# A gated long-convolution block and its feed-forward on one core: the filter's first transform turned round, its transposes moved to VectorE, and the front in a new order

## The chip, the cores and the metric

The kernel runs on one core of a Trainium2 chip. It has five engines with queues of their own: TensorE (PE in the profile; its weight loads are PEld), VectorE (DVE), ScalarE (ACT), GpSimd (POOL) and SyncE (SP), which here only issues transfers. Each works through its instructions in the order of the program and waits on semaphores where it needs another's result. The metric is the device time of one execution in microseconds (us), lower is better.

## What is computed

```python
x = A_q                                                   # 1 x 2048 x 512, float32
sa, ca, ga, sb, cb, gb = (silu(c) @ w_mod) in six rows of 512
h  = layernorm(x) * (1 + ca) + sa
ks = causal 4-tap convolution of A_k with A_shift_k, per channel
kv = ks * A_v
y  = irfft(rfft(kv, 4096) * rfft(A_ssm_k, 4096))[:2048] + kv * A_ssm_D
x  = x + ga * (h * y)
h  = layernorm(x) * (1 + cb) + sb
out = x + gb * ((silu(h @ w_gate) * (h @ w_up)) @ w_down) # 512 -> 1792 -> 512
```

There are 2048 tokens and 512 channels. The long convolution runs over tokens, for every channel, with a filter as long as the sequence; it is what the front of the kernel spends most of its time on.

## The kernel before, in words

**Two parts.** The *front* does the modulation rows, the short and the long convolution, the gate and the second normalization, and the first gate and up products; its order is written out by hand as one list of calls, from `load_k0(0)` to `next_psum()`. The *loop* is the feed-forward over 14 blocks of 128 hidden channels and two halves of the tokens, in float32 products split into three passes. The loop begins with the tile called `a`. The helper class `InOrder` keeps every engine's instructions in the order of the list, so the place of a call in the list is its place in the queue of each engine that it uses. All instructions are recorded at one line (L40), and are told apart by their tiles.

**Names.** `c_` or the first number is one of four channel blocks of 128 channels. The long convolution is a product of transforms, done in two steps of a DFT as small matrix products, for the signal X and for the filter K.

- *Short convolution:* `tap0`, `tap`, `tms`, `tma` build `u` from the four taps on ScalarE, VectorE and GpSimd; `times_v` multiplies by v. Channel block 0 arrives in another layout and has its own calls: `x0_taps`, `x0_mul`, `p_tap`, `p_mul`, `p_turn`.
- *First step for X:* `x_turn` turns 8 pieces by TensorE into the tile `kvt`, which ScalarE copies out as `x`. `x_first` multiplies by the constant DFT matrix (`raw`, tile `er`) into PSUM tile `s`, and a copy of 1024 columns stores it into X in fours, interleaved. `swap_x(n)` then turns piece n % 4 of X(n // 4) in place, 32 x 32 blocks, with VectorE's transpose.
- *First step for K:* `skip` adds the direct term D to the filter's first element (tile `ss`), so the term y += kv * D comes out of the same product. `k_first` multiplies the filter by the DFT matrix, here with the filter as the stationary operand (`s<-er,ss`). Two copies of 512 columns per call store it in KT (tile `kt`). `k_turn` then has TensorE transpose eight 128 x 128 pieces against the identity into PSUM tile `kt`, and copies them into K.
- *Second step, product and way back:* `x3` (tile `px`, two parts copied to `xs`), `x_sum` (the third part), `product3(n, m)` (TensorE makes K's second step in tile `pk`, VectorE multiplies `xs` by it), `inv3` or `inv3s` (tile `iv`, back into X; in `inv3s` VectorE's transpose does it). n runs over 8 half blocks, m over 3 parts. X(0) to X(2) are turned by a round trip to DRAM: `put` (away<-X) and `get` (X<-away).
- *Modulation:* `mod_load` brings two rows' weights (`wm`), `mod_mul` scales them by silu(c) on ScalarE, `mod_part` adds them up on GpSimd, `mod_bc` spreads the sums to all partitions by TensorE, `mod_mix` mixes them. The third pair of rows goes by `mod_row`, `mod_out` and `mod_T`.
- *Gate and second normalization:* tokens are in four quarters t. `do_stats`, `gate_n` and `gate_p` (two 512-wide instructions per token row of a partition) make the first h; `y_pe` makes the convolution's output in PSUM; `y_into` or `y_gate` and `add_y` multiply and add it to x, with the statistics of the second normalization. `rs1`, `rs2`, `rs3` finish these (VectorE, GpSimd, GpSimd), `norm1` applies them on ScalarE, `norm_t` transposes (tile `nt`), `norm_s` scales, `hi1` and `lo1` split the result in a high and a low part (tile `op`) for the products `gu_pe` (tile `g`), `gu_act` and `gu_end`.

**Room.** PSUM is handed out in four tiles of two banks (`banks`). The list `SLOTS` says which buffer each allocation takes. KT and the third weights of the modulation take turns in one buffer (`f16`, one tag with one buffer), so KT of the next channel block can be written once the last one has been read. `warm(n)` issues n products of the identity that nobody reads.

Of the kernel before, what the change touches and what calls it, by code (L numbers as in the profile page):

```python
# [43 lines left out]
def adaln_h3_swiglu(ctx, tc, q, k0, v0, kT, vT, ssm, dskip, wgu, wdn, wmod, e_fwd, e_inv, w_c, out):  # L44
# [1186 lines left out]
    room()
    tap(1, 1)
    tap(1, 2)
    skip(0, e=dve)
# [3 lines left out]
    load_v(2)
    swap_x(2)
    swap_x(3)  # L1240
    k_first(0, 2, e=act)
    k_first(0, 1, e=act)
# [1 line left out]
    k_first(0, 3, e=act)
    times_v(1, 1, e=pool)
    k_first(0, 0, e=act)
    tap0(2, e=act)
    warm(5)
    k_turn(0, 0, e=act)
    k_turn(0, 1, e=dve)  # L1250
    tap(2, 1)
    times_v(1, 0, e=pool)
    k_turn(0, 2, e=act)
    x_turn(1, 1, e=act)
    k_turn(0, 3, e=act)
    tap(2, 2)
    load_ssm(1)
# [42 lines left out]
    mod_load(0)  # L1300
    tma(3, 2, 0, e=pool)
    tma(3, 3, 0, e=pool)
    product3(0, 0)
    load_ssm(3)
    mod_mul(0, 0, e=act)
    load_ssm(2)
    product3(1, 2)
    product3(0, 1)
# [494 lines left out]
```

## Time and profile before

| What | us |
|---|---|
| three runs | 573.32, 573.87, 575.27; median 573.87 |
| the profiled execution | 574.47, span 572.7 |
| TensorE busy | 567.3 |
| VectorE busy | 436.9 |
| GpSimd busy | 330.9 |
| ScalarE busy | 301.0 |
| the front, to the loop's first product | 181.4 |

A row of groups reads: line, engine, operation, tile written <- tiles read, partitions x elements, count | busy us, mean ns of one | idle time of the engine before them and what ended it. A float32 product is recorded as two matmul passes, a transpose as one. The ends of matmuls are modelled, and the duration of one (275 ns) overlaps the next; their pace is seen in the starts and in the chain of waits. A row of a timeline reads: start, duration, engine, operation, tiles, count, and in brackets the idle time before it. The chain of waits is followed back from the last instruction, so its rows are the start and the length of each piece of work on it.

### The profile page before, as it was taken

The numbers are of one execution on the slowest core, as the hardware profiler recorded it, in microseconds if no ns is written. First come the engines' busy times: TensorE is split into PE (matmuls) and PEld (weight loads), VectorE is DVE, ScalarE is ACT, GpSimd is POOL, SyncE is SP. The second block draws the span as 40 slices with busy tenths as digits, with TensorE's granted clock in tenths as the row PEclk, the third lists the DMA queues.
The fourth block names the chain that finished last, engine by engine and source line by source line (L and its number), as shares of the span: only waits on it lengthen the run. The fifth ranks groups of instructions, "written<-read, shape, count | busy, mean of one in ns | idle before, by whom it ended". The sixth has DMA issues, their size and how long they took to land.

```text
span 572.7 us, 10192 instructions
## 1 busy us (share of the span) xinstructions
PE 567.3 (99%) x4010; PEld 450.5 (79%) x4010; DVE 436.9 (76%) x625; ACT 301.0 (53%) x459; POOL 330.9 (58%) x303
## 2 busy tenths in 40 slices
PE   9999999999999999999999999999999999999997
PEld 9985476546888888888888888887888888888886
DVE  4897896989998866676576569857686868686766
...
GB/s 318 401 289 228 383 264 240 208 255 208 76 38 201 121 247 168 228 260 62 248 285 380 170 167 0 116 198 166 129 166 129 166 128 166 129 166 129 166 0 147
DMA packets 52545, 108.00 MB, mean 189 GB/s; under 512 B 19345, under 2 KB 34065, under 8 KB 46482
## 3 DMA queue, kind: packets, MB, share of 16 engines
...
## 4 chain that ended last, share of the span: by engine, by line
PE 90%; DMA 3%; ACT 2%; DVE 2%; SPq 1%; issue 0%; POOL 0%; ACTq 0%; POOLq 0%
PE a L40 23%; PE dn L40 15%; PE c L40 12%; PE b L40 6%; PE da L40 6%; PE s L40 4%; PE g L40 4%; PE iv L40 3%; PE pk L40 3%; PE dc L40 3%; PE kvt L40 2%; DMA wm<-in_wmod 2%; PE kt L40 2%; PE px L40 2%; PE warm L40 1%; PE y L40 1%
## 5 line engine op out<-in xcount | busy, mean ns | idle before, releaser
L40 PE MATMUL a<-op,wsum 128*128 128x512 f32 x432 | 109.8, 390 | 0.0
L40 PEld LDWEIGHTS a<-op,wsum 128*128 128x128 f32 x432 | 81.0, 188 | 17.4 <-ACT p L40 0.4
L40 PE MATMUL dn<-wd,acts 128*128 128x512 f32 x336 | 84.8, 389 | 0.0
L40 PEld LDWEIGHTS dn<-wd,acts 128*128 128x128 f32 x336 | 63.1, 188 | 13.1
L40 ACT COPY p<-a 128x512 f32<-128x512 f32 x50 | 29.4, 587 | 57.7 <-PE a L40 57.7
L40 DVE TENSOR_TENSOR x<-x,dn 128x512 f32<-128x512 f32 (+1 forms) x65 | 43.2, 670 | 13.2 <-PE dn L40 12.9
L40 POOL TENSOR_TENSOR wa<-ws,wa 128x512 fp32r<-128x512 f32 (+1 forms) x28 | 32.0, 1165 | 26.2 <-ACT wa L40 26.2
L40 POOL TENSOR_TENSOR tb<-wds 128x256 f32<-128x256 f32 x12 | 8.9, 741 | 62.7 <-DVE wds L40 62.7
L40 ACT COPY r<-a 128x512 f32<-128x512 f32 x24 | 14.1, 587 | 53.8 <-PE a L40 53.8
L40 DVE TENSOR_TENSOR b<-r,c 128x512 f32<-128x512 f32 x24 | 16.7, 696 | 32.2 <-ACT sg L40 32.2
L40 POOL TENSOR_TENSOR wsum<-sr,wsum 128x512 fp32r<-128x512 f32 x28 | 40.1, 1456 | 0.0
L40 PE MATMUL c<-op,wsum 128*128 128x512 f32 x156 | 39.6, 389 | 0.0
L40 PE MATMUL c<-op,wa 128*128 128x512 f32 x156 | 39.6, 389 | 0.0
L40 PE MATMUL b<-op,wa 128*128 128x512 f32 x144 | 36.5, 389 | 0.0
L40 POOL TENSOR_TENSOR wd<-wds,wd 128x512 fp32r<-128x512 f32 x14 | 18.3, 1327 | 30.4 <-ACT wd L40 30.4
L40 PEld LDWEIGHTS c<-op,wa 128*128 128x128 f32 x156 | 29.3, 188 | 6.1
L40 PEld LDWEIGHTS c<-op,wsum 128*128 128x128 f32 x156 | 29.3, 188 | 6.1
L40 DVE TENSOR_TENSOR x<-x,da 128x512 f32<-128x512 f32 x48 | 32.7, 681 | 0.9 <-PE da L40 0.9
L40 DVE TENSOR_TENSOR xs<-pk,xs 128x1024 f32<-128x1024 f32 x24 | 27.6, 1213 | 7.3 <-PE pk L40 7.3
L40 PEld LDWEIGHTS b<-op,wa 128*128 128x128 f32 x144 | 27.0, 188 | 5.6
L40 POOL TENSOR_TENSOR s<-s,bcs 128x512 f32<-128x512 f32 x22 | 28.3, 1299 | 0.9
L40 ACT ACTIVATE sg<-a 128x512 f32<-128x512 f32 x26 | 15.5, 598 | 22.6 <-PE a L40 22.6
...
## 6 DMA issues: line engine op xcount, KB each, us to landing
...
```

Source lines behind the costliest of these rows:

```text
L40: return lambda *a, **k: self.tc.keep_in_program_order(f(*a, **k))
```

## The change

`k_first` exchanges its operands: the DFT matrix is stationary and the filter moves, as in `x_first`. What lies along the partitions of the result changes with it, and it is stored by one interleaved copy of 1024 columns. `k_turn`, with its transposes on TensorE and its copies, is gone; `k_swap(c_, i)` has VectorE transpose 32 x 32 blocks from KT to K instead, four calls of 1024 columns to a channel block. `x_first` is split in four calls of a quarter each; the work in them is the same. The long list of calls has a new order, with some calls on other engines. Calls of `mod_mul` stand on ScalarE in both.

```diff
@@ -51,11 +51,11 @@
     dp = ctx.enter_context(tc.tile_pool(name="dp", bufs=1, space=bass.MemoryType.DRAM))
 
     SLOTS = {
-        "e8": "...",
-        "b16": "...",
+        "e8": "...",
+        "b16": "...",
...
-        "ps": "...",
-        "r4": "...",
+        "ps": "...",
+        "r4": "...",
...
     }
     pps = [
@@ -281,50 +281,41 @@
         x = XT[c_, half] = r4([P, 8, P], F32, f"x{c_}{half}")
         copy(e, x, pt)
 
-    def x_first(c_, half, e=act):
-
-
-        if half == 0:
+    def x_first(c_, jq, e=act):
+
+        if c_ not in X:
             X[c_] = b16(f"X{c_}")
-        x = XT.pop((c_, half))
-        for o in range(0, 8, 4):
-            ps = banks("s1")
-            j0 = 8 * half + o
-            for jj in range(4):
-                for a in range(2):
-                    pe.matmul(
-                        ps[:, a, jj * P : (jj + 1) * P], raw[rows(a), j0 + jj], x[rows(a), o + jj], start=True, stop=True
-                    )
-            copy(e, fours(X[c_])[:, j0 // 4 :: 4], ps.rearrange("p a (f d) -> p a d f", f=4))
-
-
-    def k_first(c_, jq, e=act):
-
-        if c_ not in KT:
-            KT[c_] = f16(f"kt{c_}", (P, 4, 32, 32))
+        x = XT[c_, jq // 2]
         ps = banks("s1")
         for jj in range(4):
             for a in range(2):
                 pe.matmul(
-                    ps[:, a, jj * P : (jj + 1) * P], SS[c_][rows(a), 4 * jq + jj], raw[rows(a), 4 * jq + jj],
+                    ps[:, a, jj * P : (jj + 1) * P], raw[rows(a), 4 * jq + jj], x[rows(a), (4 * jq + jj) % 8],
                     start=True, stop=True,
                 )
-        for a in range(2):
-            j = J * a + 4 * jq
-            copy(
-                e, KT[c_][:, :, j : j + 4, :].rearrange("p g j k -> p j g k"),
-                ps[:, a].rearrange("p (j g k) -> p j g k", j=4, g=4),
-            )
-
-    def k_turn(c_, m, e=act):
-
-        if m == 0:
+        copy(e, fours(X[c_])[:, jq::4], ps.rearrange("p a (f d) -> p a d f", f=4))
+
+    def k_first(c_, jq, e=act):
+
+        if c_ not in KT:
+            KT[c_] = f16(f"kt{c_}", (P, 32, P))
+        ps = banks("s1")
+        for jj in range(4):
+            for a in range(2):
+                pe.matmul(
+                    ps[:, a, jj * P : (jj + 1) * P], raw[rows(a), 4 * jq + jj], SS[c_][rows(a), 4 * jq + jj],
+                    start=True, stop=True,
+                )
+        copy(e, fours(KT[c_])[:, jq::4], ps.rearrange("p a (f d) -> p a d f", f=4))
+
+    def k_swap(c_, i):
+
+        if c_ not in K:
             K[c_] = b16(f"K{c_}")
-        ps = banks("kt").rearrange("p a (k d) -> p (a k) d", k=4)
-        src = KT[c_].rearrange("p g j k -> p (g j) k")
-        for k in range(8):
-            pe.transpose(ps[:, k], src[:, :, 8 * m + k], ident)
-        copy(e, fours(K[c_])[:, 2 * m : 2 * m + 2], ps.rearrange("p (g f) d -> p g d f", f=4))
+        r = slice(32 * i, 32 * i + 32)
+        dve.transpose(
+            fours(K[c_])[:, :, r].rearrange("p g d f -> p d g f"), fours(KT[c_])[:, :, r].rearrange("p g d f -> p d g f")
+        )
 
     def fours(t):
 
```

The new list, in order, from the start to where the loop's buffers are set up. A call without a name behind it runs on its only engine or on ScalarE; the calls behind it (`wd_lo` to `next_psum`) are those of before.

```
load_k0(0); diag(0); warm(5); diag(1); diag(2) DVE; load_dskip(); warm(16); diag(3); load_k0(1); p_tap0() DVE; p_tap(1,1) DVE; p_tap(1,0)
DVE; p_tap(2,0) DVE; load_k(1); p_tap(2,1) DVE; x0_taps(0); p_tap(3,1) DVE; load_v0(0); load_v0(1); x0_mul(0); load_e(0); load_ssm(0,0);
small_in(); silu_c(); tap0(1); load_e(2); load_ssm(0,2); load_e(1); p_tap(3,0) DVE; p_mul(0) DVE; p_mul(1) POOL; x0_taps(1); x_first(0,0);
load_e(3); load_ssm(0,1); p_turn(); skip(0) POOL; tap(1,1); k_first(0,2); x0_mul(1); tap(1,2); tap(1,3); x_first(0,1); x_first(0,3);
x_first(0,2); swap_x(1); load_ssm(0,3); k_first(0,3); load_v(1); times_v(1,0) POOL; k_first(0,0); k_first(0,1); times_v(1,1) POOL;
load_k(2); tap0(2); swap_x(0); load_wc(); swap_x(2); times_v(1,3) POOL; load_ssm(1); times_v(1,2) POOL; k_swap(0,0); k_swap(0,1);
x_turn(1,0); x3(0,2); x3(0,1); x_turn(1,1); x_sum(0) POOL; k_swap(0,3); k_swap(0,2); k_first(1,3); x_first(1,0); x_first(1,1); skip(1) POOL;
swap_x(3); x3(1,1); x3(1,2); tap(2,1); tap(2,2); tap(2,3); load_ssm(3); k_first(1,1); load_k(3); skip(3) POOL; k_first(1,2); x_sum(1) POOL;
load_v(2); x_first(1,2); x_first(1,3); times_v(2,0) POOL; tms(3,2); mod_rep() DVE; product3(1,2); tap0(3) DVE; tap(3,1); times_v(2,1) POOL;
times_v(2,2) POOL; mod_load(1); product3(1,1); mod_load(0); k_first(1,0); x_turn(2,0); room(); product3(0,2); product3(0,1); tms(3,3);
load_x(1); times_v(2,3) POOL; product3(0,0); tma(3,2,2) POOL; tma(3,2,1) POOL; tma(3,2,0) POOL; product3(1,0); mod_mul(0,0); mod_part(0,0)
POOL; x_first(2,0); x_first(2,1); k_swap(1,0); k_swap(1,1); x_turn(2,1); mod_mul(0,1); tma(3,2,3) POOL; tma(3,3,3) POOL; load_x(0);
k_swap(1,2); do_stats(1,0); mod_part(0,1) POOL; inv3(1); load_ssm(2); skip(2) POOL; inv3(0); x_first(2,2); x_first(2,3); swap_x(6);
swap_x(5); swap_x(4); x3(2,2); swap_x(7); x3(3,2); do_stats(0,0); tma(3,3,0) POOL; k_swap(1,3); swap_x(10); load_v(3); mod_part(0,2) DVE;
x3(3,1); x3(2,1); k_first(2,0); k_first(2,1); k_first(2,2); k_first(2,3); swap_x(11); swap_x(9); tma(3,3,2) POOL; swap_x(8); put(0);
tma(3,3,1) POOL; times_v(3,0) POOL; times_v(3,1) POOL; x_sum(3) POOL; product3(3,2); product3(3,1); x_turn(3,0); product3(3,0); x_sum(2)
POOL; product3(2,0); product3(2,2); load_x(2); mod_mul(1,1); product3(2,1); mod_part(0,3) POOL; load_x(3); mod_mul(1,0); k_swap(2,0);
k_swap(2,2); times_v(3,2) POOL; get(0); mod_part(1,1) POOL; times_v(3,3) DVE; do_stats(2,0); inv3(3); inv3(2); x_turn(3,1); k_swap(2,3);
put(1); x3(5,2); mod_part(1,0) POOL; mod_part(1,2) POOL; x3(5,1); k_swap(2,1); x_first(3,0); x_first(3,2); mod_part(1,3) POOL; x_sum(5)
POOL; x_first(3,1); do_stats(0,1); x3(4,2); do_stats(3,0); do_stats(3,1); x3(4,1); do_stats(2,1); product3(5,1); x_sum(4) POOL;
product3(5,0); product3(5,2); gate_n(0,0); x_first(3,3); swap_x(13); k_first(3,1); do_stats(1,1); swap_x(15); k_first(3,2); mod_bc(1);
mod_bc(0); k_first(3,3); load_einv(); k_first(3,0); gate_n(0,1); mod_mix(); gate_p(0,1,1) POOL; gate_p(0,0,1) POOL; product3(4,1);
product3(4,2); gate_n(2,0); gate_p(0,2,1) POOL; gate_p(0,3,1) POOL; product3(4,0); gate_n(2,1); swap_x(14); swap_x(12); k_swap(3,0);
k_swap(3,3); k_swap(3,2); inv3(5); inv3(4); x3(7,2); gate_p(2,0,1) DVE; x3(7,1); x_sum(7) POOL; k_swap(3,1); get(1); y_pe(0,0,1);
gate_n(3,1); x3(6,1); warm(5); y_into(0,0,1); x3(6,2); x_sum(6) POOL; load_w(1); product3(7,1); product3(7,0); put(2); product3(7,2);
gate_n(1,0); gate_n(1,1); product3(6,1); gate_p(2,3,1) POOL; product3(6,2); gate_p(2,1,1) POOL; w8_hi(1); product3(6,0); gate_p(1,1,1) POOL;
inv3s(7); inv3s(6); y_pe(2,0,1); gate_p(2,2,1) POOL; gate_n(3,0); y_gate(2,0,1); gate_p(1,0,1) POOL; mod_load(2,0); mod_row(2,0);
gate_p(1,3,1) POOL; mod_load(2,1); y_pe(1,0,1); y_pe(0,3); gate_p(1,2,1) DVE; mod_row(2,1); get(2); y_pe(0,2); mod_out(2); y_pe(2,2,3);
y_into(0,3); y_into(0,2); rs1(0); y_gate(2,2,3); load_w(0); mod_T(); w8_lo(1) POOL; w8_hi(0); rs2(0); rs3(0); norm1(0,0); w8_lo(0) POOL;
y_pe(1,2,3); y_into(1,0,1); y_into(1,2,3); norm1(0,1); norm1(0,2); norm1(0,3); y_pe(3,0,1); norm_t(0,0); norm_s(0,0); hi1("B11",0);
acts_room(); rs1(1); norm_t(0,1); y_pe(3,2,3); lo1("B11",0) POOL; norm_s(0,1); hi1("B11",1); norm_t(0,2); lo1("B11",1) DVE; gate_p(3,1,1)
POOL; gate_p(3,0,1) DVE; norm_t(0,3); gu_pe(0,0,0); rs2(1); gate_p(3,2,1) DVE; norm_s(0,2); rs3(1); norm_s(0,3); hi1("B21",0); gate_p(3,3,1)
DVE; y_gate(3,2,3); lo1("B21",0) POOL; norm1(1,0); norm1(1,1); hi1("B21",1); norm1(1,2); room(); add_y(3,0,4,(2,3)) POOL; gu_pe(1,0,0);
gu_pe(1,0,1); gu_pe(0,0,1); load_w(2); norm1(1,3); load_w(3); lo1("B21",1) DVE; y_gate(3,0,1); add_y(3,0,4,(0,1)) DVE; gu_pe(0,0,2);
gu_pe(1,0,2); norm_t(1,0); norm_t(1,1); norm_s(1,0); hi1("B12",0); gu_pe(1,0,3); norm_t(1,2); norm_t(1,3); norm_s(1,1) DVE; gu_act(1,0);
norm_s(1,2); hi1("B22",0) DVE; hi1("B12",1); gu_pe(0,0,3); norm_s(1,3); hi1("B22",1); lo1("B12",0) POOL; load_wd(0); wd_mul(0) DVE;
lo1("B12",1) POOL; gu_act(0,0); add_y(2,0,4,(0,1)) DVE; wd_hi(0); diff("B11","B12","B11") POOL; gu_end(1,0); gu_end(0,0); lo1("B22",0) DVE;
room(); gu_pe(0,1,0); lo1("B22",1) DVE; op_hi("T1","B11"); diff("B12","B22","B12") DVE; op_hi("T3","B12"); add_y(2,0,4,(2,3)) POOL;
first_downs(); next_sbuf()
```

More of the change, by code (lines that the diff above doesn't have):

```diff
@@ L1224, in adaln_h3_swiglu @@
+    tap(1, 1)
+    k_first(0, 2, e=act)
     x0_mul(1)
-    x_first(0, 0, e=act)
+    tap(1, 2)
+    tap(1, 3)
     x_first(0, 1, e=act)
-    load_ssm(0, 1)
-    load_ssm(0, 2)
+    x_first(0, 3, e=act)
+    x_first(0, 2, e=act)
+    swap_x(1)
     load_ssm(0, 3)
+    k_first(0, 3, e=act)
     load_v(1)
[L1231 to L1234, printed above, removed]
+    times_v(1, 0, e=pool)
+    k_first(0, 0, e=act)
+    k_first(0, 1, e=act)
+    times_v(1, 1, e=pool)
     load_k(2)
-    tap(1, 3)
+    tap0(2, e=act)
@@ L1237, in adaln_h3_swiglu @@
+    swap_x(0)
+    load_wc()
+    swap_x(2)
     times_v(1, 3, e=pool)
[L1238 to L1242, printed above, removed]
-    times_v(1, 2, e=pool)
[L1244 to L1257, printed above, removed]
@@ L1300, in adaln_h3_swiglu @@
[L1300 to L1308, printed above, removed]
-    product3(0, 2)
-    product3(1, 0)
-    k_turn(1, 2, e=act)
-    x_first(2, 1, e=act)
-    swap_x(7)
-    swap_x(5)
-    load_v(3)
-    mod_load(1)
-    swap_x(8)
-    mod_part(0, 0, e=pool)
-    load_x(0)
-    tma(3, 3, 2, e=pool)
-    load_einv()
-    times_v(3, 1, e=pool)
-    skip(2, e=dve)
-    mod_mul(0, 1, e=act)
@@ L1325, in adaln_h3_swiglu @@
-    times_v(3, 2, e=pool)
-    inv3(1, e=act)
-    inv3(0, e=act)
-    put(0)
-    load_x(2)
-    load_x(3)
-    times_v(3, 3, e=pool)
-    k_turn(1, 1, e=act)
-    swap_x(10)
-    x3(3, 2, e=dve)
-    x3(2, 1, e=act)
-    x3(3, 1, e=act)
-    swap_x(9)
-    skip(3, e=dve)
-    times_v(3, 0, e=pool)
-    k_first(2, 0, e=act)
-    k_first(2, 2, e=act)
-    x_sum(3, e=dve)
-    get(0)
-    x3(2, 2, e=act)
-    x_sum(2, e=pool)
-    mod_mul(1, 0, e=act)
-    mod_part(1, 0, e=pool)
-    product3(3, 2)
@@ L1349, in adaln_h3_swiglu @@
-    product3(3, 0)
-    product3(3, 1)
-    mod_mul(1, 1, e=act)
+    x_turn(1, 1, e=act)
+    x_sum(0, e=pool)
+    k_swap(0, 3)
+    k_swap(0, 2)
+    k_first(1, 3, e=act)
+    x_first(1, 0, e=act)
+    x_first(1, 1, e=act)
+    skip(1, e=pool)
+    swap_x(3)
+    x3(1, 1, e=act)
+    x3(1, 2, e=act)
+    tap(2, 1)
+    tap(2, 2)
+    tap(2, 3)
+    load_ssm(3)
+    k_first(1, 1, e=act)
+    load_k(3)
+    skip(3, e=pool)
+    k_first(1, 2, e=act)
+    x_sum(1, e=pool)
+    load_v(2)
+    x_first(1, 2, e=act)
@@ new lines, in adaln_h3_swiglu @@
+    x_first(1, 3, e=act)
+    times_v(2, 0, e=pool)
+    tms(3, 2, e=act)
+    mod_rep(e=dve)
+    product3(1, 2)
+    tap0(3, e=dve)
+    tap(3, 1)
+    times_v(2, 1, e=pool)
+    times_v(2, 2, e=pool)
+    mod_load(1)
+    product3(1, 1)
+    mod_load(0)
+    k_first(1, 0, e=act)
+    x_turn(2, 0, e=act)
+    room()
+    product3(0, 2)
+    product3(0, 1)
+    tms(3, 3, e=act)
+    load_x(1)
+    times_v(2, 3, e=pool)
+    product3(0, 0)
+    tma(3, 2, 2, e=pool)
+    tma(3, 2, 1, e=pool)
+    tma(3, 2, 0, e=pool)
@@ new lines, in adaln_h3_swiglu @@
+    product3(1, 0)
+    mod_mul(0, 0, e=act)
+    mod_part(0, 0, e=pool)
+    x_first(2, 0, e=act)
+    x_first(2, 1, e=act)
+    k_swap(1, 0)
+    k_swap(1, 1)
+    x_turn(2, 1, e=act)
+    mod_mul(0, 1, e=act)
+    tma(3, 2, 3, e=pool)
+    tma(3, 3, 3, e=pool)
+    load_x(0)
+    k_swap(1, 2)
+    do_stats(1, 0)
+    mod_part(0, 1, e=pool)
+    inv3(1, e=act)
+    load_ssm(2)
+    skip(2, e=pool)
+    inv3(0, e=act)
+    x_first(2, 2, e=act)
+    x_first(2, 3, e=act)
+    swap_x(6)
+    swap_x(5)
@@ new lines, in adaln_h3_swiglu @@
+    swap_x(4)
+    x3(2, 2, e=act)
+    swap_x(7)
+    x3(3, 2, e=act)
+    do_stats(0, 0)
+    tma(3, 3, 0, e=pool)
+    k_swap(1, 3)
+    swap_x(10)
+    load_v(3)
+    mod_part(0, 2, e=dve)
+    x3(3, 1, e=act)
+    x3(2, 1, e=act)
+    k_first(2, 0, e=act)
+    k_first(2, 1, e=act)
+    k_first(2, 2, e=act)
+    k_first(2, 3, e=act)
+    swap_x(11)
+    swap_x(9)
+    tma(3, 3, 2, e=pool)
+    swap_x(8)
+    put(0)
+    tma(3, 3, 1, e=pool)
+    times_v(3, 0, e=pool)
+    times_v(3, 1, e=pool)
@@ L1352, in adaln_h3_swiglu @@
+    x_sum(3, e=pool)
+    product3(3, 2)
+    product3(3, 1)
+    x_turn(3, 0, e=act)
+    product3(3, 0)
+    x_sum(2, e=pool)
     product3(2, 0)
     product3(2, 2)
[L1354 to L1362 removed]
+    load_x(2)
+    mod_mul(1, 1, e=act)
+    product3(2, 1)
+    mod_part(0, 3, e=pool)
+    load_x(3)
@@ L1363, in adaln_h3_swiglu @@
+    mod_mul(1, 0, e=act)
+    k_swap(2, 0)
+    k_swap(2, 2)
+    times_v(3, 2, e=pool)
+    get(0)
+    mod_part(1, 1, e=pool)
+    times_v(3, 3, e=dve)
+    do_stats(2, 0)
     inv3(3, e=act)
     inv3(2, e=act)
-    do_stats(2, 0)
-    k_turn(2, 0, e=act)
     x_turn(3, 1, e=act)
-    k_turn(2, 1, e=act)
-    k_turn(2, 3, e=act)
-    swap_x(11)
+    k_swap(2, 3)
     put(1)
-    get(1)
+    x3(5, 2, e=act)
+    mod_part(1, 0, e=pool)
+    mod_part(1, 2, e=pool)
+    x3(5, 1, e=act)
+    k_swap(2, 1)
@@ L1524, in adaln_h3_swiglu @@
     gu_pe(0, 0, 1)
+    load_w(2)
+    norm1(1, 3, e=act)
     load_w(3)
-    norm1(1, 3, e=act)
+    lo1("B21", 1, e=dve)
+    y_gate(3, 0, 1)
+    add_y(3, 0, 4, (0, 1), e=dve)
     gu_pe(0, 0, 2)
+    gu_pe(1, 0, 2)
     norm_t(1, 0)
     norm_t(1, 1)
-    add_y(2, 0, 4, (2, 3), e=dve)
     norm_s(1, 0, e=act)
     hi1("B12", 0, e=act)
+    gu_pe(1, 0, 3)
     norm_t(1, 2)
```

308 lines of the change are left out of this document (134 added, 174 removed).

## The prediction

> **What bounds the kernel now.** I read the page's totals first, then TensorE's waits, then busy time by stage.
>
> ```profile
> span 572.7 us, 10192 instructions
> PE 567.3 (99%) x4010; PEld 450.5 (79%) x4010; DVE 436.9 (76%) x625; ACT 301.0 (53%) x459; POOL 330.9 (58%) x303
> ...
> PE warm L40 <- POOL ident masks.py:199: 1.3, 1, 1.3
> PE mr L40 <- DMA wm<-in_wmod: 0.3, 1, 0.3
> ```
>
> After its start TensorE waits nowhere longer than 0.3 us: it sets the pace everywhere, so work taken from it should be time. Whether it is depends on how far behind it the others are. The stage view (columns: stage, its length, then busy time of PE, PEld, DVE, ACT, POOL, the clock, DMA share, GB/s) says that:
>
> ```profile
> 0.00:40.00 40.00, 38.44 (x438) 37.72 (x439) 30.12 (x30) 28.46 (x41) 13.49 (x15) 1.00 0.91 351
> 40.00:153.90 113.90, 113.58 (x1736) 70.50 (x1735) 98.57 (x150) 91.05 (x117) 96.17 (x88) 1.00 0.82 238
> 153.90:181.40 27.50, 27.50 (x131) 22.98 (x130) 25.68 (x30) 15.83 (x24) 15.88 (x13) 1.00 0.23 72
> 181.40:572.70 391.30, 387.81 (x1711) 319.32 (x1709) 282.56 (x417) 165.71 (x279) 205.41 (x190) 1.00 0.48 166
> ```
>
> I chose the two cuts at these rows of VectorE's and TensorE's timelines and of the chain of waits:
>
> ```profile
> 153.64 0.24 DVE L40 TENSOR_SCALAR rsb<-mvb 128x4 f32<-128x4 f32 x2
> ...
> 159.06 1.91 PE L40 MATMUL nt<-ident,n 128*128 128x128 f32 x16
> ...
> 181.41 1.36 PE a L40 x6
> ```
>
> At 153.9 VectorE finishes `rs1(1)`, the statistics of the second token quarter. Through POOL's power and ScalarE's `norm1` they release `norm_t(1, 0)` at 159.06, which comes just in time for TensorE, and 27.5 us after 153.9 the feed-forward loop starts at 181.4. From there on 391.3 us are untouched by the diff. So the front is worth 181.4 us, and VectorE is busy 30.1 + 98.6 = 128.7 of the 153.9 us to `rs1(1)`: idle 25.2, of which 9.9 before 40 us and 15.3 after it. That idle time is the whole cover for what the change gives VectorE.
>
> **The change part by part.** The prices, by groups:
>
> ```profile
> L40 PE MATMUL kt<-ident,kt 128*128 128x128 f32 x128 | 16.8, 282 | 0.2 <-ACT kt L40 0.2
> L40 PE MATMUL s<-x,er 64*128 64x128 f32 x256 | 15.9, 275 | 0.0
> L40 PE MATMUL s<-er,ss 64*128 64x128 f32 x256 | 15.7, 275 | 0.0
> L40 DVE STREAM_TRANSPOSE X<-X 128x1024 f32<-128x1024 f32 x16 | 19.1, 1218 | 1.5 <-ACT X L40 1.5
> L40 DVE STREAM_TRANSPOSE X<-iv 128x1024 f32<-128x1024 f32 x4 | 7.5, 2084 | 0.0
> L40 DVE TENSOR_TENSOR s<-s,bcs 128x512 f32<-128x512 f32 x10 | 7.5, 780 | 0.2
> L40 DVE TENSOR_TENSOR xs<-xs 128x512 f32<-128x512 f32 x2 | 2.3, 1183 | 0.0
> L40 DVE COPY K<-kt 128x1024 f32<-128x1024 f32 x1 | 1.2, 1225 | 1.7 <-PE kt L40 1.7
> L40 DVE COPY xs<-px 128x1024 f32<-128x1024 f32 x1 | 1.2, 1225 | 2.3 <-PE px L40 2.3
> L40 DVE TENSOR_TENSOR ss<-ss,bcs 1x128 f32<-1x128 f32 x3 | 2.0, 651 | 0.0
> L40 DVE TENSOR_SCALAR s<-x,rsa 128x512 f32<-128x512 f32 x2 | 1.0, 534 | 0.0
> L40 ACT COPY kt<-s 128x512 f32<-128x512 f32 x32 | 16.9, 691 | 0.3 <-PE s L40 0.2
> L40 ACT COPY X<-s 128x1024 f32<-128x1024 f32 x16 | 16.1, 1110 | 0.1
> L40 ACT COPY K<-kt 128x1024 f32<-128x1024 f32 x15 | 15.7, 1094 | 0.7 <-PE kt L40 0.7
> ```
>
> *TensorE.* The 128 transposes of `k_turn` go. In the chain 24 take 2.96 us, so 0.123 each and 15.8 in all (the group's 16.8 counts modelled ends too). `k_first` only exchanges its operands; the old form (15.7) stands beside `x_first`, which already has the new one (15.9), so it costs nothing more. Of the warm-up calls, 16 + 5 instead of 16 stand at the start and 5 still near the end. The net for TensorE is -15.8.
>
> ```profile
> 24.71 2.96 PE kt L40 x24
> ...
> 1.34 4.85 PE L40 MATMUL warm<-ident 128*128 128x128 f32 x21 [1.34 <-POOL ident masks.py:199]
> ```
>
> *ScalarE.* Fifteen copies out of the transposes go (-15.7); `k_first` stores one 1024-wide piece in the form of the X copies instead of two 512-wide ones (16.9 to 16.1). Single copies and normalizations moved to it add about 3. It has slack after 40 us. `mod_mul` is on ScalarE in both orders, so that part of the change moves nothing between engines; it only comes earlier.
>
> *VectorE, to `rs1(1)`.* Sixteen `k_swap` calls of the shape of the X swap. The trace shows no block transpose between two buffers; the bounds are 1.19 each (SBUF in place, 19.1/16) and 1.88 (7.5/4, from PSUM). I take 1.19, since only the destination differs: +19.1; the upper end would add 11. `mod_part(0, 2)` comes with two 512-wide sums of 0.7 (the 0.78 row, uncontended 0.68): +1.4. Taken off it: the K copy 1.2, an `x3` copy 1.2, an `x_sum` 2.3, three `skip` 2.0, a `gate_n` 1.0, and three of the five `gate_p` that stood ahead of `rs1(1)`, 3 x 1.5 = 4.5. Net +8.3: VectorE must be busy 137.0 us by `rs1(1)`.
>
> So TensorE alone could be at `norm_t(1, 0)` some 14 us earlier (15.8 less one `gu_pe` call, six products of 0.23, now ahead of it), and VectorE's own work rules that out. With the statistics 5.2 us ahead of `norm_t` as now, a full gain needs `rs1(1)` at 153.9 - 15.8 = 138.1, after 137.0 of work; VectorE cannot start before 4.9. **The pace of the front passes to VectorE**, and the time follows its idle time.
>
> *Its idle time in the new order,* walked along the queues with these durations.
>
> ```profile
> 4.86 0.29 DVE L40 TENSOR_SCALAR dg<-ident,k 128x128 f32<-128x128 f32 x1 [3.70 <-DMA k<-in_k]
> 6.11 0.75 DVE L40 TENSOR_SCALAR u<-k 128x1024 f32<-128x1024 f32 x1 [0.96 <-DMA k<-in_k]
> 11.43 0.69 DVE L40 TENSOR_TENSOR x<-kvt,v 128x512 f32<-128x512 f32 x1 [0.89 <-PE kvt L40]
> ```
>
> It waits 4.9 for the first rows of k and 1.0 for the second half. In `x0_mul(0)` it waits 1.9: 0.9 as now, and the taps come 1.1 later behind ten more warm-up passes (two to a call) at 0.11 to 0.12. In the first X swap it waits 1.1, for ScalarE completes X(0) at about 22.8. That is 8.9 before 40 us. After that the K swaps fill the gaps which VectorE now spends waiting for the products: K(1) is swapped right behind the first products, K(2) behind the next. I get the last product of pieces 2 and 3 at 76 (now 77.3), `y_into(0, 0, 1)` at about 112 and the end of the last inverse transposes at 130; waits there come to about 2, at `product3(5, 1)` and `mod_mix`, where ScalarE's copies come last.
>
> ```profile
> 117.67 1.23 DVE L40 TENSOR_TENSOR y<-y,s 128x1024 f32<-128x1024 f32 x1 [1.33 <-ACT s L40]
> ...
> 135.78 1.34 DVE L40 TENSOR_TENSOR s<-y,s 128x1024 f32<-128x1024 f32 x1
> ...
> 112.19 0.34 SPq L40 DMA_DIRECT2D away<-X  x1
> 119.18 7.11 SPq L40 DMA_DIRECT2D X<-away  x4
> 126.34 3.46 SPq L40 DMA_DIRECT2D wm<-in_wmod  x1
> ...
> 126.34 12.29 DMA wm<-in_wmod
> ```
>
> *The moved loads.* v0 is now sent behind k(1): 2.8 MB ahead of its first half at 0.35 MB per us (351 GB/s in the first stage) is about 8 us, plus a start of some 2, and it is wanted at 12.5. `load_dskip` ahead of k's second half is 2 KB. `mod_load(1)` and `(0)` follow `load_v(2)`, which is free to go at about 28.5: 5 MB at 0.31 to 0.35 end at 43 to 45, and ScalarE's `mod_mul(0, 0)` wants them at about 47, so 2 us cover them; were they later, the copies of X(2) queued behind that call would be late too. `load_w(1)` is moved ahead of `put(2)`, and both halves of `mod_load(2)` ahead of `get(2)` on SP. So X(2)'s return becomes the last of that group, which now lands at 126.34 + 12.29 = 138.6. X(2) leaves about 3 us earlier, hence about 135.6, against 134.7 when VectorE wants `y_into(0, 2)` (one TensorE product later, 0.9): +2, and 1 more where transfers overlap. Total idle 8.9 + 2 + 3 = 14: `rs1(1)` at 151.0, 2.9 earlier.
>
> *Behind it:*
>
> ```profile
> L40 POOL TENSOR_TENSOR s<-s,bcs 128x512 f32<-128x512 f32 x22 | 28.3, 1299 | 0.9
> ```
>
> Three `gate_p` (4.5) now stand on VectorE behind `rs1(1)`; two `add_y`, a `diff` and two `lo1`, eight 512-wide pieces at 1.3, stand on POOL (+10.4), and what VectorE gives away so makes up for the `gate_p`. By the stage rows VectorE stays near 26 of the 27.5 us and POOL goes from 15.9 to 26. TensorE has 22.3 us from `norm_t` on, so both just fit beside it. I keep 27.5; without that cover it is 1 to 2 more, for `lo1("B22", 0)`, which `gu_pe(0, 1, 2)` needs, and `split_w(2)`, which the loop needs, stand last in the two queues.
>
> **Sum.** 572.7 - 2.9 = 569.8 of span; the profiled execution took 574.47 with 1.77 around its span, and the median of the three runs is 573.87, 0.6 below it: 569.8 + 1.8 - 0.6 = **571.0**.
>
> **Rivals.**
> *VectorE never starves.* Its idle time after 40 us shrinks to 1: `rs1(1)` at 147, -6.9, **567.0**. For it: it has 9 us more work, so fewer gaps. Below 563 it can't go by much: that needs a shorter tail as well. All of TensorE's 15.8 would give 558; the 137.0 speak against it.
>
> *The single K buffer, the slower side.* `f16` has one buffer, so the first K copy of the next block waits on ScalarE for the fourth `k_swap` of the last one, with the X copies queued behind it, PSUM fills, TensorE stops, and VectorE waits for products:
>
> ```profile
> DVE xs L40 <- PE pk L40: 7.3, 3, 3.6
> ```
>
> At up to 3.6 a hand-over, three hand-overs add 10.8 to the idle 14: `rs1(1)` at 161.8, **581.8**. It decides from 16.9 idle on (153.9 - 137.0), so from the first full hand-over: one alone gives 574.6. Against it: by my walk the swaps end 1 to 3 us ahead of the copies each time. Without that lead every microsecond is paid.
>
> *VectorE and POOL hold each other up.* One tap takes 3.36 where its neighbour took 2.34, under POOL's `times_v`:
>
> ```profile
> 32.88 2.34 DVE L40 SCALAR_TENSOR_TENSOR u<-kt,sm,u 128x2045 f32<-128x2045 f32 x1
> 39.28 3.36 DVE L40 SCALAR_TENSOR_TENSOR u<-kt,sm,u 128x2047 f32<-128x2047 f32 x1
> ```
>
> Nine taps, the products with rows and sums are of this kind; three more hits of 1.0 on VectorE's path, since it no longer has idle time to absorb them, give **574**. The Trainium skill has this as a rule in SBUF — State Buffer, "Who interferes with whom": VectorE's instructions with two SBUF inputs and a GpSimd instruction that reads SBUF exclude each other for the whole instruction. The 3.36 agrees; the K swaps have one input and would be exempt.
>
> *TensorE goes slow in its new gaps.* The first 21 matmuls took 4.85 us, 0.231 each, against 0.124 later, at a granted clock of 1.00. If a gap brings that state back while TensorE sets the pace, about 2.3 are lost (4.85 - 21 x 0.123): **573.3**. TensorE: Matmul & The Clock Gate, "What's actually happening", of the Trainium skill says half rate follows an idle window of about 3.4 us; no run here shows such a gap yet.
>
> *A K swap costs what the PSUM one does:* +11, **582**.
>
> **How the numbers follow.** Chances: forecast 0.46 (its own range 567.5 to 573.5), never starved 0.16, single buffer 0.18, ports 0.09, slow gaps 0.08, dear swaps 0.03. What can be told from no change is 0.3%, 1.7 us. Faster: 0.40 of the forecast, the 0.16 and 0.02 of the slow gaps, 0.58. Slower: 0.16 of the single buffer, 0.03 of the swaps, 0.02 of the ports, 0.21. The rest, 0.21, is the same. The range holds the unstarved case with a shorter tail (563) and two of the three hand-overs (578).
>
> **What would show it.** TensorE shows waits for VectorE or ScalarE of some 12 us, mostly ahead of `nt` and `g`, and its `kt` group is gone; VectorE is above 90% busy from 25 us to `rs1(1)`; sixteen K transposes at 1.19; `rs1(1)` near 151 and the loop's start near 178.5. It is wrong if TensorE still waits for nothing, if `rs1(1)` comes after 154, or if the 391.3 us behind the loop's start change.

## The result, and the profile after

The changed kernel took **583.17 us** (median of four: 581.64, 583.15, 583.19, 583.36) against 573.6 before (with a fourth run, 573.22), a ratio of 1.0155 [1.0129, 1.0182]: slower by 1.6%, where 571.0 was forecast, and above the range (563 to 578). The profiled execution took 581.64. The other three had a span about 1.6 us longer at a mean granted clock of 0.988 instead of 0.991, which fits one more stretch of 3.4 us at half clock; the readings below are of the profiled one.

The page's totals and the head of its chain:

```profile
span 579.9 us, 9903 instructions
PE 560.0 (97%) x3882; PEld 435.5 (75%) x3882; DVE 460.8 (79%) x630; ACT 290.2 (50%) x431; POOL 348.5 (60%) x310
...
PE 74%; DVE 21%; issue 2%; ACT 2%; POOL 0%; DVEq 0%; ACTq 0%; POOLq 0%
```

TensorE was 90% of the chain before; now a fifth of it is VectorE. Busy time by stage, with the cuts at the same two events (end of `rs1(1)`, the loop's first product on the chain; columns as in the prediction):

```profile
0.00:40.00 40.00, 38.43 (x482) 33.02 (x482) 32.87 (x28) 28.38 (x32) 17.77 (x18) 1.00 0.97 381
40.00:152.70 112.70, 103.38 (x1562) 59.17 (x1560) 111.36 (x155) 78.22 (x95) 97.30 (x86) 0.97 0.75 220
152.70:188.50 35.80, 30.29 (x133) 24.12 (x132) 33.74 (x32) 17.82 (x27) 27.85 (x18) 0.95 0.25 82
188.50:579.90 391.40, 387.87 (x1710) 319.24 (x1709) 282.87 (x417) 165.81 (x279) 205.57 (x190) 1.00 0.48 166
```

The loop is what it was, 391.4 us. `rs1(1)` ends at 152.7, 1.2 earlier than before. **The whole loss of the profiled execution, 7.2 us of span, lies in the tail**, between `rs1(1)` and the loop: 35.6 us (to 188.3, where the record of the loop's first product starts, 0.2 ahead of its place on the chain) instead of 27.4. GpSimd's busy time there is 27.9 instead of 15.9, VectorE's 33.7 instead of 25.7.

TensorE's waits from 20 us to the loop (engine, tile waited for; us in total, times, longest):

```profile
PE g L40 <- DVE op L40: 5.4, 1, 5.4
PE kvt L40 <- POOL vt L40: 4.4, 3, 3.1
PE y L40 <- DVE y L40: 1.9, 1, 1.9
PE pk L40 <- DVE xs L40: 1.5, 2, 1.2
PE nt L40 <- ACT hraw L40: 0.9, 1, 0.9
```

The first of them is the tail's: a gate product waits 5.4 us for a low part (`lo1`) from VectorE. What delays VectorE is seen in the groups of its tail, before (153.9 to 181.3) and after (152.7 to 188.3); the last columns are count, busy us and mean ns of one.

```profile
L40 DVE TENSOR_TENSOR x<-x,s 128x1024 f32<-128x1024 f32 x4 | 5.3, 1338 | 0.0
L40 DVE TENSOR_TENSOR op<-hraw,op 128x512 fp32r<-128x512 f32 x6 | 4.6, 766 | 0.1
L40 DVE TENSOR_TENSOR acts<-sg,acts 128x512 fp32r<-128x512 f32 x3 | 2.5, 864 | 0.7 <-ACT acts L40 0.7
L40 DVE TENSOR_TENSOR sg<-sg,g 128x512 f32<-128x512 f32 x4 | 2.6, 677 | 1.1 <-ACT sg L40 1.1
```

```profile
L40 DVE TENSOR_TENSOR acts<-sg,acts 128x512 fp32r<-128x512 f32 x3 | 5.2, 1753 | 0.7 <-ACT acts L40 0.7
L40 DVE TENSOR_TENSOR x<-x,s 128x1024 f32<-128x1024 f32 x2 | 5.0, 2504 | 0.0
L40 DVE TENSOR_TENSOR op<-hraw,op 128x512 fp32r<-128x512 f32 x4 | 3.7, 948 | 0.1
L40 DVE TENSOR_TENSOR wds<-wds,bcs 128x1024 f32<-128x1024 f32 x1 | 2.3, 2318 | 0.0
L40 DVE TENSOR_TENSOR sg<-sg,g 128x512 f32<-128x512 f32 x4 | 2.7, 677 | 1.1 <-ACT sg L40 1.1
```

The same instruction with both inputs in SBUF takes about twice as long (1338 to 2504, 864 to 1753), while one with an input in PSUM (`sg<-sg,g`) takes 677 in both. The timeline of the changed kernel puts GpSimd's sums right beside the long ones (start, us, engine):

```profile
168.27 2.83 DVE L40 TENSOR_TENSOR x<-x,s 128x1024 f32<-128x1024 f32 x1
168.75 1.14 ACT L40 CAST acts<-sg 128x512 fp32r<-128x512 f32 x2
169.98 3.33 POOL L40 TENSOR_TENSOR x<-x,s 128x1024 f32<-128x1024 f32 x1
...
171.03 3.96 DVE L40 TENSOR_TENSOR acts<-sg,acts 128x512 fp32r<-128x512 f32 x2
...
176.17 4.14 PE L40 MATMUL g<-op,wg 128*128 128x512 f32 x11 [5.37 <-DVE op L40]
```

VectorE's `acts` pair, 1.28 in the same place before, takes 3.96: its first half waits out GpSimd's half of `add_y`, which ends at 173.31. In the text below **stretch** is the sum, over VectorE's instructions, of the duration less the shortest duration of the same operation and shape in the traces, where instructions that read PSUM count as a shape of their own. Before it was 8.2 us to `rs1(1)` and 2.5 in the tail; after, 13.5 and 10.5. How finely shapes are told apart moves each of these sums by up to 0.9, and their growth by up to 0.4. VectorE's busy time less its stretch in the tail is 23.1 before and 23.0 after, its idle time there 1.8 and 2.1. So in VectorE's queue the tail's +8.2 is stretch, +8.0.

On the chain of waits it is two things. VectorE leads from ahead of `rs1(1)` until the low part is done, and then TensorE leads at half clock:

```profile
171.11 3.88 DVE acts L40 x2
174.99 1.14 DVE op L40
176.13 0.04 issue
176.17 4.14 PE g L40 x11
180.32 1.37 PE dn L40 x6
181.69 2.72 PE g L40 x12
```

Eleven such products take 2.5 at full clock (twelve take 2.72 in the last row), so by this estimate some 6.7 of the 8.2 come from VectorE's lateness and 1.5 from the half clock that follows TensorE's wait. That this adds up to nearly VectorE's stretch is no proof by itself; the experiments below have to show the cause.

### The profile page after: what moved, and what is told of

Its sections match the earlier page's. It is cut to its first block, busy times and chain, and to the rows that moved or that the text cites. A ratio compares the mean times of both kernels' runs of the same rounds, so it can differ in the third digit from the quotient of the medians.

```text
span 579.9 us, 9903 instructions
## 1 busy us (share of the span) xinstructions
PE 560.0 (97%) x3882; PEld 435.5 (75%) x3882; DVE 460.8 (79%) x630; ACT 290.2 (50%) x431; POOL 348.5 (60%) x310
## 4 chain that ended last, share of the span: by engine, by line
PE 74%; DVE 21%; issue 2%; ACT 2%; POOL 0%; DVEq 0%; ACTq 0%; POOLq 0%
PE a L40 23%; PE dn L40 15%; PE c L40 12%; PE b L40 6%; PE da L40 6%; DVE X L40 3%; DVE xs L40 3%; PE dc L40 3%; DVE K L40 2%; DVE s L40 2%; DVE x L40 2%; PE kvt L40 2%; DVE u L40 2%; DVE bna L40 1%; PE warm L40 1%
## 5 line engine op out<-in xcount | busy, mean ns | idle before, releaser
L40 ACT COPY r<-a 128x512 f32<-128x512 f32 x24 | 14.1, 587 | 53.7 <-PE a L40 53.5
L40 PE MATMUL b<-op,wa 128*128 128x512 f32 x144 | 36.5, 389 | 0.0
L40 PE MATMUL g<-op,wg 128*128 128x512 f32 x96 | 25.1, 414 | 5.5 <-DVE op L40 5.4
## 6 DMA issues: line engine op xcount, KB each, us to landing
wm<-in_wmod SPq DMA_DIRECT2D x6, 1024.0 KB, 10.1
```

The costliest lines, as they stand in the source:

```text
L40: return lambda *a, **k: self.tc.keep_in_program_order(f(*a, **k))
```

## The experiments

Theory A: VectorE paces the front, and what it loses to GpSimd's sums (they exclude each other) lengthens the tail. (In some of the expectations that are quoted, A names only its first half, the amount of VectorE's work.) Theory B: GpSimd costs VectorE nothing; the order, the waits or the clock make the loss. The table has what all runs gave (us; ratios to the kernel before beside each run).

| kernel | median | `rs1(1)` ends | tail | stretch in the tail |
|---|---|---|---|---|
| before | 573.6 | 153.9 | 27.4 | 2.5 |
| after | 583.2 | 152.7 | 35.6 | 10.5 |
| k_all_old | 588.0 | 167.9 | 27.4 | 2.6 |
| k0_old | 574.9 | 154.1 | 27.4 | 2.5 |
| k01_old | 582.4 | 161.3 | 27.4 | 2.6 |
| k2_old | 576.7 | 155.5 | 27.4 | 2.5 |
| k3_old | 579.4 | 157.9 | 27.4 | 2.5 |
| k_twice | 595.8 | 166.5 | 36.0 | 10.9 |
| k_copy_act | 586.0 | 154.6 | 36.2 | 10.4 |
| mix23 | 598.5 | 168.8 | 36.5 | 9.7 |
| tail_dve | 581.1 | 155.1 | 33.8 | 5.5 |
| lo1_first | 584.2 | 152.6 | 38.2 | 11.0 |
| lo1_first_dve | 581.9 | 153.8 | 36.7 | 6.2 |
| warm_fill | 582.5 | 152.6 | 36.8 | 10.8 |
| before_tt | 577.5 | 153.8 | 31.1 | 5.6 |
| before_ms | 574.0 | 153.7 | 27.5 | 3.0 |
| tail_out | 578.2 | 151.3 | 31.9 | 4.7 |

**One part alone: the exchange of engines in the old order** (`k_all_old`, and block by block). The edit to the kernel before is the new `k_first` and, for the blocks named,

```diff
-    k_turn(0, 0, e=act)
+    k_swap(0, 0)
```

> The order of before, in it only the K path of the change: all 16 k_turn calls become k_swap at the same places, k_first in its new form. Theory A (VectorE's own amount of work sets the front): it must be busy 128.7 + 19.1 - 1.2 = 146.6 us by rs1(1) and idles at least 9.9 before 40 us, so rs1(1) comes at 156.5 or later against 153.9, and the time is 576 to 582. Theory B (the K path is good by itself and the new order spoils it): TensorE's 15.8 us come through in large part, 560 to 568.

> The order of before, only channel block 0's K turned by VectorE (4 of 16 calls). TensorE loses 32 transposes, 3.9 us; VectorE gets 3.6 more, into gaps of 25 us. If TensorE sets the pace of before and VectorE's gaps can be filled: 570 (-3.5 to -3.9). If the statistics rs1(1), which came just in time, move with VectorE's work: 574 to 577.

> The order of before, K of channel blocks 0 and 1 turned by VectorE. TensorE loses 7.9 us, VectorE gets 8.3: busy 137.0 by rs1(1). By VectorE's amount with 9.9 idle early it can't have rs1(1) before 147, which is 146 us (153.9 - 7.9) on TensorE's side: 566 to 569 if its gaps fill, 574 to 578 if the order does not let it fill them.

Measured: 587.95, 1.0249 [1.0233, 1.0265]; 574.87, 1.0032 [1.0020, 1.0043]; 582.42, 1.0153 [1.0128, 1.0178]. Only block 0 alone came out as expected; the other two lie 6 and 4 us above both of their expectations. TensorE's largest waits of `k0_old`, `k01_old` and `k_all_old`:

```profile
PE kvt L40 <- POOL vt L40: 2.3, 2, 1.3
```

```profile
PE kvt L40 <- POOL vt L40: 8.6, 3, 6.4
```

```profile
PE kvt L40 <- POOL vt L40: 9.5, 3, 7.2
PE pk L40 <- DVE xs L40: 3.7, 1, 3.7
PE pk L40 <- DVE x L40: 3.4, 1, 3.4
```

Without the new order the tail stays at 27.4 and `rs1(1)` goes up to 14 us later. Block 0 alone saves TensorE 3.9 us, and 3.7 come back as its waits from 20 us on, 2.3 of them for the taps that VectorE does 1.5 later, by way of GpSimd's `times_v`. The amount of VectorE's work does not explain `k_all_old`: it is busy 146.6 us by `rs1(1)`, as expected, and idle 21.3. In the old order the engines then wait for each other, and it isn't VectorE's amount that sets `rs1(1)`. So the exchange by itself costs time; the new order wins it back ahead of `rs1(1)` and loses in the tail.

Two later runs took the other blocks, in whose time VectorE had some room (2) and none (3):

> The kernel before in its own order, K of block 2 alone turned by VectorE: TensorE loses 32 transposes (3.9 us), VectorE gets 4 of 1.19 (4.8) between 100 and 120 us, where it has 2.3 us idle. Theory A (worth what VectorE has idle there): between 1.5 us faster and 2 slower, 572 to 576. If TensorE's saving counts in full, as TensorE is busy all the time there: 570.

> The same for block 3 alone, whose turns stand where VectorE has 0.5 us idle in 20 and ScalarE is nearly empty. Theory A: 4.8 more on a full VectorE, 2.5 to 5 slower, 576 to 579. If TensorE's saving counts in full: 570.

Measured: 576.69, 1.0046 [1.0024, 1.0068], and 579.40, 1.0086 [1.0065, 1.0107], each 0.4 to 0.7 above its expectation's upper end, in the expected order. TensorE's first two waits of `k3_old`:

```profile
PE pk L40 <- DVE x L40: 3.9, 1, 3.9
PE pk L40 <- DVE K L40: 1.9, 1, 1.9
```

None of the blocks tried alone (0, 2 and 3; 1 was exchanged only together with others) brings a gain at its old place: TensorE's saving counts in none of them.

**Is VectorE's amount the pace?** To the changed kernel:

```diff
-        dve.transpose(
...
+        for _ in range(2 if c_ else 1):
+            dve.transpose(
...
```

> The changed kernel with each K transpose of blocks 1, 2 and 3 done twice (the second writes the same again): VectorE gets 12 more of 1.19, 14.3 us, no other engine gets any. Theory A (VectorE paces the front behind 40 us, where it has 1.4 us idle in the changed kernel): rs1(1) from 152.7 to 165 to 167, the tail as it was (35 to 36), 595 to 598. Theory B (GpSimd and ScalarE hold the middle equally, VectorE's queue only looks full because it is stretched and waits elsewhere): rs1(1) at 153 to 159, 583 to 590.

Measured: 595.83, 1.0376 [1.0357, 1.0395]. The stage between 40 us and `rs1(1)`:

```profile
40.00:167.00 127.00, 108.35 (x1571) 61.27 (x1567) 124.20 (x168) 79.31 (x96) 96.21 (x87) 0.93 0.69 198
```

14.3 us more on VectorE alone move `rs1(1)` by 13.8, with VectorE (third busy column) at 124.2 of 127 and the tail at 36.0. Theory A holds for this direction: more work on VectorE is paid. Two runs tried the other direction and could not show it. In the first ScalarE copies KT to K and nothing is turned:

```diff
-        dve.transpose(
-            fours(K[c_])[:, :, r].rearrange("p g d f -> p d g f"), fours(KT[c_])[:, :, r].rearrange("p g d f -> p d g f")
-        )
+        act.copy(fours(K[c_])[:, :, r], fours(KT[c_])[:, :, r])
```

> The changed kernel with the 16 block transposes of K replaced by plain copies of the same pieces on ScalarE, at the same places: the filter isn't turned, so this part of the convolution is left out, and VectorE is free of 19.1 us. Theory A (VectorE's amount of work sets the front): rs1(1) comes 12 to 19 us earlier, and with an unchanged rest of 35 us the time is 565 to 571. If something else holds the front (TensorE's waits for GpSimd, the transfers, ScalarE, which gets 16.8 more), less than 6 us come off: 577 or more.

Measured: 586.03, 1.0219 [1.0202, 1.0236]; `rs1(1)` at 154.6. Theory A's expectation was missed, the gain of 12 to 19 us didn't come: VectorE now waits, for sums that GpSimd makes of ScalarE's late copies (its waits from 40 us):

```profile
DVE xs L40 <- POOL xs L40: 5.3, 1, 5.3
DVE xs L40 <- PE pk L40: 5.0, 4, 4.0
```

ScalarE and the chain through GpSimd stand close behind VectorE, so the 19.1 us taken from VectorE and put on ScalarE (16.8) were worth nothing. In the second, TensorE turns blocks 2 and 3 again:

```diff
-    k_swap(2, 0)
...
+    k_turn(2, 0, e=act)
...
```

> The changed kernel in its new order, but K of blocks 2 and 3 is turned by TensorE as before: VectorE loses 8 transposes of 1.19 (9.5 us), TensorE gets 64 transposes of 0.123 (7.9), ScalarE 8 evictions of 1.1 to 1.3. If the amount of VectorE's work sets the front: rs1(1) from 152.7 to 145 to 149, 575 to 580. If VectorE, ScalarE and GpSimd hold the middle equally, as the run with copies on ScalarE suggests: rs1(1) stays at 152 to 156, 582 to 586. The tail stays at 35 to 36 by both.

Measured: 598.53, 1.0430 [1.0414, 1.0447], far outside both expectations. The transposes stand where VectorE's swaps stood in the list, and TensorE now waits for ScalarE's copies of them; the longest of these waits:

```profile
PE kt L40 <- ACT K L40: 2.9, 1, 2.9
```

It says nothing of VectorE's amount: VectorE is idle 25.7 us between 40 and `rs1(1)`, and the 16 us by which `rs1(1)` comes later aren't taken apart here. How much a VectorE relieved without loading another engine would gain stays open.

**What makes the tail long.** First, by itself: in the kernel before, work that nobody reads is put on GpSimd behind `lo1("B21", 0, e=pool)`, once with two SBUF inputs and once with none. The kernel's own work stays as it is.

```diff
+    scratch = f16("scratch", (P, 512))
+    pool.memset(scratch, 0.0)
+    for _ in range(4):
+        pool.tensor_tensor(scratch, scratch, scratch, op=ALU.add)
```

> The kernel before, with one fill and four sums of a scratch tile with itself (128x512, 1.30 us each where such a one stands alone) on GpSimd behind its first low part of B21, where GpSimd is idle for 4.43 us; nothing reads the scratch tile. Theory A (an operation of GpSimd that reads SBUF holds up one of VectorE with two inputs in SBUF): VectorE is 99% busy there, so its stretch in the tail rises from 2.5 by 3 to 5, the loop starts 3 to 5 us later (184.3 to 186.3), 577 to 579. Theory B (GpSimd's sums cost VectorE nothing, the tail after the change is long by its order and its waits): the loop starts at 181.3 to 182, 573.9 to 574.5.

```diff
+    scratch = f16("scratch", (P, 512))
+    pool.memset(scratch, 0.0)
+    for _ in range(8):
+        pool.memset(scratch, 0.0)
```

> The same place and about the same GpSimd time, but nine fills of the scratch tile (no input) in place of the fill and four sums. Theory A as the Trainium skill has it (SBUF — State Buffer, section Who interferes with whom: only against a GpSimd operation that reads SBUF): no stretch, loop start 181.3 to 182, 574. If any work of GpSimd holds VectorE up: as the kernel with the sums, 577 to 579. Theory B: 574.

Measured: 577.54, **1.0062** [1.0046, 1.0077], and 573.97, **1.0001** [0.9992, 1.0011]. The timelines, with the sums and then with the fills:

```profile
156.88 5.98 POOL L40 TENSOR_TENSOR scratch<-scratch 128x512 f32<-128x512 f32 x4
...
159.90 4.04 DVE L40 TENSOR_TENSOR x<-x,s 128x1024 f32<-128x1024 f32 x2
```

```profile
156.18 5.21 POOL L40 MEMSET scratch<- 128x512 f32 x9
```

The two `x<-x,s`, 2.35 in the kernel before, take 4.04 under the sums. The loop starts 3.6 later, of which 3.1 is stretch. 5.2 us of fills in the same place cost nothing. So it is not GpSimd's being busy or late, but its sums' reading of SBUF, that holds VectorE up. Theory B falls for GpSimd's part; the clock is looked at below.

Then the changed kernel without GpSimd's three large sums in the tail, so that it leaves out a part of the result:

```diff
-    add_y(3, 0, 4, (2, 3), e=pool)
...
-    add_y(2, 0, 4, (2, 3), e=pool)
...
-    diff("B11", "B12", "B11", e=pool)
```

> The changed kernel without GpSimd's three large sums behind the second rs1: both halves (2, 3) of add_y for rows 3 and 2 (the gated product isn't added to half of x there) and the difference for T1 (B11 is used as it is). VectorE's own work is not touched. Theory A: VectorE's stretch in the tail falls from 10.5 to 4 to 5.5, so the tail from 35.6 to 29 to 31, loop start 182 to 184, 575 to 577.5. Theory B: the tail stays at 34 to 36, 581 to 583.

Measured: 578.16, 1.0072 [1.0052, 1.0091]. Two groups of its tail:

```profile
L40 DVE TENSOR_TENSOR acts<-sg,acts 128x512 fp32r<-128x512 f32 x3 | 3.6, 1228 | 0.7 <-ACT acts L40 0.7
L40 DVE TENSOR_TENSOR x<-x,s 128x1024 f32<-128x1024 f32 x2 | 2.8, 1389 | 0.0
```

The stretch falls by 5.8 as expected, the tail by 3.7 to 31.9, 0.9 above the expectation: some 2 us come back as waits of VectorE for ScalarE (`sg`, 3.0 instead of 1.1). The tail stays 4.5 longer than before the change: 2.2 of that is stretch beside GpSimd's other sums, read from the trace and not tried, and TensorE still goes through 3.4 us of half clock there. And the same three sums on VectorE:

```diff
-    add_y(3, 0, 4, (2, 3), e=pool)
+    add_y(3, 0, 4, (2, 3), e=dve)
...
-    diff("B11", "B12", "B11", e=pool)
+    diff("B11", "B12", "B11", e=dve)
...
-    add_y(2, 0, 4, (2, 3), e=pool)
+    add_y(2, 0, 4, (2, 3), e=dve)
```

> The changed kernel with three of the sums that it moved to GpSimd behind rs1(1) (both add_y on columns 2 and 3, and diff of B11) back on VectorE, nothing else. Theory A (amount): VectorE gets 2 x 2.4 + 1.2 = 6.0 us more behind rs1(1), where it sets the pace: 588 to 589. Theory C (VectorE's instructions with two SBUF inputs wait for GpSimd's, 10.5 us of stretch behind rs1(1)): most of that stretch goes, the 6.0 come, and the time is 579 to 583.

Measured: 581.08, 1.0127 [1.0108, 1.0147]. The stretch falls by 5.0, VectorE's own work rises by 3 x 1.2 = 3.6 (my 6.0 counted each `add_y` twice), and the tail falls by 1.8 to 33.8. `rs1(1)` came 2.4 later in this profile, which the edit, behind it, does not explain.

**The wait itself.** The calls that make TensorE's 5.4 us wait end were put ahead of VectorE's other work, alone and together with the last edit:

```diff
+    lo1("B22", 0, e=dve)
+    lo1("B22", 1, e=dve)
     load_wd(0)
     wd_mul(0, e=dve)
...
-    lo1("B22", 0, e=dve)
...
-    lo1("B22", 1, e=dve)
```

> The changed kernel with lo1 of B22 (both halves) put ahead of wd_mul, add_y and gu_end in VectorE's queue, nothing else. In the changed kernel TensorE waits 5.4 us for it at 176 and then runs 3.4 us at half clock. Theory D (the place in VectorE's queue behind rs1(1) makes the late start): gu_pe finds its operand at about 168, the wait goes and the loop starts 4 to 7 us earlier: 576 to 579. Theory A (VectorE's amount of work behind rs1(1) makes it): the wait moves to the next consumer (wd_lo, gu_end) and the time stays at 582 to 584.

> Both: lo1 of B22 ahead, and both add_y and the diff back on VectorE (which alone gave 581.1, stretch behind rs1(1) 10.5 to 5.5 us at 3.6 us more of own work). If place and mutual exclusion are two separate terms, they add up: 573 to 577. If each only frees what the other one holds, 578 to 581.

Measured: 584.20, 1.0185 [1.0165, 1.0206], and 581.94, 1.0152 [1.0134, 1.0169]; the second lies 0.9 above the larger of its two expectations. Theory D's gain came in neither. In the tail of the first, TensorE waits once, later and longer:

```profile
PE dn L40 <- DVE wd L40: 6.5, 1, 6.5
```

So the place of `lo1` isn't what makes the tail long: what VectorE owes before the loop had to be done in this order too.

**The clock.** After a gap in TensorE's work the granted clock falls (`warm(14)` ahead of `x_turn(2, 0)` fills the gap):

```diff
+    warm(14)
     x_turn(2, 0, e=act)
```

> The changed kernel with 14 more products of the identity ahead of x_turn(2, 0), in the place where TensorE waits 3.1 and 1.1 us for GpSimd's times_v and its granted clock is then 0.5 for 6.8 us. Theory E (the slow stretch costs time): the clock stays at 1.00 from 40 to 50 us, the products there take 3.5 us instead of 5.1, and 1 to 1.5 us are gained: 581.5 to 582.3. Theory A (VectorE sets the pace there, TensorE's slow stretch lies beside it): the clock stays up and the time stays, 582.8 to 583.6.

Measured: 582.48, 1.0152 [1.0131, 1.0172], between the two expectations, so the time does not tell them apart; the stage does. Busy time between 40 and 50 us, after and with the filling (the clock is the number behind the five engines):

```profile
40.00:50.00 10.00, 5.79 (x50) 2.46 (x56) 9.78 (x8) 4.90 (x5) 8.14 (x5) 0.66 0.24 97
```

```profile
40.00:50.00 10.00, 8.68 (x116) 6.20 (x116) 9.96 (x7) 5.31 (x4) 7.72 (x5) 1.00 0.27 115
```

The clock stays at 1.00, and `rs1(1)` ends at 152.6 as without it: half rate cost nothing here, where VectorE sets the pace. The second stretch, in the tail, was not tried by itself; the 1.5 of it is the estimate from the chain above.

None of these versions is faster than the kernel before.

## Why the prediction failed

**Right:** *VectorE's swap price*. It was 1.19 by choice against an upper bound of 1.88. It takes what the X swap takes:

```profile
L40 DVE STREAM_TRANSPOSE X<-X 128x1024 f32<-128x1024 f32 x16 | 18.8, 1213 | 0.3 <-ACT X L40 0.3
...
L40 DVE STREAM_TRANSPOSE K<-kt 128x1024 f32<-128x1024 f32 x16 | 18.7, 1210 | 0.0
```

*The pace passes to VectorE.* It does: it is idle 1.3 of the 112.7 us between 40 and `rs1(1)`, and `k_twice` shows that added work there is paid nearly one to one. *TensorE's waits of some 12 us*: 14.1 in the rows shown, but ahead of `g` and `kvt` (the latter for GpSimd) rather than `nt`. *The loop's 391.3*: 391.4. *The single K buffer* held nothing up: ScalarE has no wait on a swap, and the rival's 581.8 was near the time for another reason.

**Right by two errors:** `rs1(1)` at 151.0, measured 152.7. Busy 137.0 became 144.2 and idle 14 became 8.5. The moved loads and the waits at `product3(5, 1)` and `mod_mix` were given 5 us, and VectorE's idle time after 40 us was 1.3, what the rival *VectorE never starves* had, because it ran behind everything that it was to wait for. The busy time has two parts. Its own work rose by 10.2 (120.5 to 130.7), not 8.3: the removed sums, `skip` and `gate_p` were taken off at about the means of their rows (1183, 651 and 780 ns), which held stretch, where undisturbed they take 0.67, 0.27 and 0.64. And the stretch rose from 8.2 to 13.5. The sum had no term for it. That the two errors cancelled to within 1.7 us is luck.

**The step that failed is "Behind it":** "I keep 27.5". The tail took 35.6, and these 8.1 are most of the 10.1 us of span that the sum missed; `rs1(1)` gives 1.7 more. (The other 2 of the 12.2 between 571.0 and 583.17 lie outside the profiled execution: the sum took 0.6 off for the median, and the median came 1.5 above the profile.) Its count of work was right: what VectorE gives away does make up for the three `gate_p` (23.1 and 23.0 without stretch), and GpSimd went to 27.9 where 26 was written. Wrong was the conclusion "both just fit beside it". Two queues of 26 us in 27.5 fit only if they run at once, and here they could only in part: what GpSimd got are sums of two SBUF tiles, and most of VectorE's tail (some 28 of 33.7 busy us) has two SBUF inputs. "Without that cover it is 1 to 2 more" should have been 8.

**The rival that named the cause was priced too low.** "VectorE and POOL hold each other up" counted three hits of 1.0 from one tap of 3.36 and had 0.09. The stretch rose by 13.3 in all, 5.3 ahead of `rs1(1)` (seen in the trace, and not tried by itself) and 8.0 behind it. One hit isn't limited to 1.0 either: a tap that takes 2.33 in the kernel before took 4.91, as it stood behind two of GpSimd's `x_sum` sums (it ended 2.15 after the second).

```profile
36.82 4.91 DVE L40 SCALAR_TENSOR_TENSOR u<-kt,sm,u 128x2045 f32<-128x2045 f32 x1
```

```profile
37.06 2.51 POOL L40 TENSOR_TENSOR xs<-xs 128x512 f32<-128x512 f32 x2
```

With the measured tail in place of 27.5 the sum would have been 151.0 + 35.6 + 391.3 = 577.9 of span, 579 in all, and the sign right. How much of the 8 us the rows of before would have given isn't shown. The Trainium skill's rule, in SBUF — State Buffer, "Who interferes with whom", says that a VectorE instruction with two SBUF inputs and a GpSimd instruction that reads SBUF shut each other out for the whole instruction. The runs agree, its exception for GpSimd instructions that read nothing too (1.0062 with sums, 1.0001 with fills). The prediction cited it and then used it on the front alone.

*Slow gaps* came about as that rival had it, but cost next to nothing ahead of `rs1(1)` and, by the estimate from the chain, 1.5 in the tail.
